# Row patches of the last quads on the GpSimd queue, and dummy matmuls in the slots of quads 13 to 15

## Chip, cores and metric

The kernel runs on one core of one Trainium2 chip. The metric is the device time of one execution in microseconds. Before the change it was 457.0 us, the median of 6 runs (455.99 to 459.12). The profiled execution took 457.49 us.

## What is computed

The input is q, k, v of shape 8 x 8 x 576 x 64, the spectral weights w_r and w_i (64 modes, 512 x 512 each) and w_ch (512 x 512), all in fp32. The first half is attention with a linear distance bias inside a window of 128 tokens. The second half mixes channels in the Fourier domain along the tokens:

```python
attn = softmax(where(0 <= rel < 128, q @ k.T / 8 - slope[h] * rel, -1e9)) @ v
x = attn.transpose(0, 2, 1, 3).reshape(8, 576, 512)
X = np.fft.rfft(x, axis=1)
Xr, Xi = X.real[:, :64], X.imag[:, :64]
Yr = einsum('bmd,mde->bme', Xr, w_r) - einsum('bmd,mde->bme', Xi, w_i)
Yi = einsum('bmd,mde->bme', Xr, w_i) + einsum('bmd,mde->bme', Xi, w_r)
Y[:, :64] = Yr + 1j * Yi          # all other modes are zero
u = x + np.fft.irfft(Y, n=576, axis=1)
out = u + maximum(u @ w_ch, 0)
```

The two spectral weights are 2 x 64 matrices of 1 MB each, so their reading takes a large part of the time.

## The kernel before

The attention stage comes first, and while it runs some spectral weights are already read. It leaves x and its spectrum XC in SBUF. The spectral stage then takes the weights in order of k = 2m + ri, where m is the mode and ri chooses w_r or w_i. A weight matrix is one load of 1 MB. Most loads go through the SyncE queue (`load_w`, L443, the issue in L456) into a ring of buffers. A weight that was just used makes room for one that comes eight later, so in the loop each slot first runs its matmuls and then issues a later load.

The loop at L791 runs over 16 quads g of four modes, and inside it over i = 0 to 7, so k = 8g + i. A slot runs four matmuls of 128x512 (L823) that add into one accumulator `acc`; each mode fills 32 of its rows (16 for the real part and 16 for the imaginary part, 8 batches each). In the last quad (g = 15, `LAST`) modes 60 and 61 go to an accumulator of their own, `half_acc`, and modes 62 and 63 are also computed transposed into `accT` by 16 small matmuls a slot (L817). After its weight, a slot has room for one more piece of work:

- `quads`: the end of an earlier quad. `quad_end` scales the accumulator (L586) and transposes it into YT. For the late quads `late_end` does it (L543 to L566): VectorE scales `acc` into a tile yq (L547), `scatter` copies its rows to the spectrum Z by DMA (L548), TensorE transposes yq (L552), and VectorE copies the transposes (L555, L560). `late_end` is called for g = 14 with four modes (56 to 59) and, after i = 3 of g = 15, for two modes (60 and 61). For g = 14 it goes on to `late_channels` (L568): four matmuls with wch, a ScalarE copy into a tile yw (L575), and `scatter` into ZW.
- `side`: from quad 8 on, 22 pieces, one on each odd slot. Four are `spectra` of the first half of the modes, 18 are `project` of one unit of tokens each (L671; its 16 matmuls are L683). The last runs on k = 107. At the end of quad 13, four more `spectra` are put in (L607, L616, copies into Z in L622); the first of them does nothing.

`scatter` (L631) issues six DMAs, one for each of batches 2 to 7. Each has 8 rows of 1 KB, or 4 rows where two modes are patched. Before the change the patches into Z go out on SyncE (L548 and L877), the patches into ZW on GpSimd (L576).

yq and yw share a tag with two buffers in the pool `fin` (bufs=2, L532). So a new one waits until one of the two last tiles is done with, its DMA reads included.

Before k = 127 the psum pool of the loop is closed, and the first matmuls of the output stage run (`begin(0)` and `add_tokens(0)`, L808 and L809). After the loop the last two modes are scaled (L872 to L876) and patched into Z (L877), then the step list of L889 forms the outputs: `activate(j)` uses ZW, `finish(j)` uses Z, and each result is written to the output by SyncE. The patch into ZW for quad 15 is issued inside `activate(0)`. The order of instructions on each engine, SyncE included, is the order of the program.

Of the kernel before, what the change touches and what calls it, by code (L numbers as in the profile page):

```python
# [10 lines left out]
FP32 = mybir.dt.float32  # L11
# [9 lines left out]
P = 128  # L21
# [379 lines left out]
def kernel(  # L401
# [10 lines left out]
    nc = tc.nc  # L412
    ctx.enter_context(tc.manual_schedule(engines=ALL | {SP}))
    B, H, S, _ = q.shape
    NM, DM, _ = moe_w_r.shape
# [8 lines left out]
    ident = const.tile([P, P], BF16, name="ident")  # L424
# [34 lines left out]
    with ExitStack() as actx:  # L459
        at = _Attention(tc, actx, q, k, v, (ident, F, FT), x, XC, raw)  # L460
        n = len(at.units)
# [11 lines left out]
        wt = at.ps.tile([P, P], FP32, tag="av", bufs=1, name="warm")  # L473
# [29 lines left out]
        for h in (0, 2):  # L503
# [4 lines left out]
        side = {0: [(at.offset, 4), (at.offset, 6), (at.decay, 5), (at.offset, 5), (at.decay, 7),  # L508
                    (at.offset, 7), (at.decay, 4), (at.decay, 6)]}
        lags = [lag for _, _, lag in STAGE]  # L510
        for stage in range(min(lags), n + max(lags)):
# [8 lines left out]
            if stage in AHEAD:  # L520
                if stage:
                    b, g = at.units[stage - 1]
# [5 lines left out]
    with ExitStack() as mctx:  # L528
# [11 lines left out]
        ps = pctx.enter_context(tc.tile_pool(name="fps", bufs=2, space=PSUM))  # L540
        heads, free = {}, []

        def late_end(acc, g, n):  # L543

            rows, m0 = slice(0, 32 * n), 4 * (g % 8)
            yq = pool.tile([P, DM], BF16, tag="yq")
            nc.vector.tensor_scalar_mul(yq[rows], acc[rows], 2.0 / S)  # L547
            scatter(nc.sync, yq, g, 0, 2 * n, lambda b: Z[:, b])  # L548
            yield
            tr = ps.tile([P, 4, P], BF16, tag="tr", bufs=1, name="tr")  # L550
            for et in range(4):
                nc.tensor.transpose(tr[:, et, rows], yq[rows, et * P : (et + 1) * P],  # L552
                                    ident[rows, rows])
            for ri in range(2):
                nc.vector.tensor_copy(  # L555
                    YT[:, 1, :, :2, m0 : m0 + n, ri],
                    tr[:, :, rows].rearrange("p e (j c) -> p e c j", c=32)[
                        :, :, 16 * ri : 16 * ri + 2])
            yT = pool.tile([P, 2, 4, P], BF16, tag="xT", name="xT")[:, 0]
            nc.vector.tensor_copy(yT[:, :, rows], tr[:, :, rows])  # L560
            heads[g] = yq, yT
            if n < 4:
                return
            yield
            zw = ps.tile([P, DM], FP32, tag="zw", bufs=1, name="zw")
            late_channels(g, zw, yT)  # L566

        def late_channels(g, zw, yT):  # L568
            for et in range(4):
                nc.tensor.matmul(zw, lhsT=yT[:, et], rhs=wch[:, et],  # L570
                                 start=(et == 0), stop=(et == 3))

            def patch():
                yw = pool.tile([P, DM], BF16, tag="yq")
                nc.scalar.copy(yw, zw)  # L575
                scatter(nc.gpsimd, yw, g, 0, 8, lambda b: ZW[:, b // 2, 1])  # L576

            if g == LAST:
                heads["patch"] = patch
            else:  # L580
                patch()
# [49 lines left out]
        def scatter(queue, rows, g, lo, hi, dst):  # L631

            for b in range(2, B):
                r = 64 * (b % 2) + 8 * (g % 8)
                queue.dma_start(out=dst(b)[r + lo : r + hi],  # L635
                                in_=rows.rearrange("(k v) e -> k v e", v=16)[lo:hi, b])
# [19 lines left out]
        def token_tiles(j):  # L656
            b, st = units[j]
            return x[:, b : b + 2, st] if st < FULL else x[:, b + 1 : b + 4 : 2, FULL]
# [3 lines left out]
        def transposed(j):  # L662
            src = token_tiles(j)
            tr = ps.tile([P, 2, 4, P], BF16, tag="tr", bufs=1, name="tr")
            for n in range(2):
                for dt in range(4):
                    nc.tensor.transpose(tr[:, n, dt], src[:, n, dt * P : (dt + 1) * P], ident)  # L667
            xTs[j] = pool.tile([P, 2, 4, P], BF16, tag="xT", name="xT")
            nc.vector.tensor_copy(xTs[j], tr)  # L669

        def project(j):  # L671

# [114 lines left out]
        quads, side, recycle = [], [], list(again)  # L787
        ZW = Z = XW = wch = w2 = None
        K1 = again[-1] + 1
        LAST = NM // 4 - 1  # L790
        for g in range(NM // 4):  # L791
            acc = (lps if g % 2 else ps).tile([P, DM], FP32, tag="acc", bufs=1, name="acc")
            if g == LAST:
                half_acc = ps.tile([P, DM], FP32, tag="z", bufs=1, name="z")
                accT = lps.tile([P, 4, 2, 32], FP32, tag="accT", name="accT")
            for i in range(8):
                m, ri = 4 * g + i // 2, i % 2
                if 2 * m + ri not in wq:
                    continue
                w = wq[2 * m + ri]  # L800
                if 2 * m + ri == 2 * NM - 1:
                    assert not side and not quads
                    pctx.close()
                    head = mctx.enter_context(
                        tc.tile_pool(name="hps", bufs=1, space=PSUM, reuse_waits="tile"))
                    heads.update(mm=[head], yy=[head])
                    free.append(0)
                    begin(0)  # L808
                    add_tokens(0)  # L809
                window = []  # L810
                for a in range(4):
                    c0 = (a // 2 * 2 * NC + 16 * (1 - ri) + a % 2 * 8) * NM + m
                    window.append(XC[:, c0 : c0 + 31 * NM + 1 : NM])
                into = half_acc if g == LAST and i < 4 else acc
                for a in range(4 if g == LAST and i >= 4 else 0):
                    for et in range(4):
                        nc.tensor.matmul(  # L817
                            accT[:, et, i // 2 - 2], lhsT=w[a][:, et * P : (et + 1) * P],
                            rhs=window[a], start=(i == 4 and a == 0 and et == 0),
                            stop=(i == 7 and a == 3 and et == 3), skip_group_check=True,  # L820
                        )
                for a in range(4):
                    nc.tensor.matmul(  # L823
                        into[32 * (i // 2) : 32 * (i // 2) + 32],
                        lhsT=window[a],
                        rhs=w[a],
                        start=(ri == 0 and a == 0), stop=(ri == (m > 0) and a == 3),
                        tile_position=(0, 32 * (i // 2)),
                    )
                k = 8 * g + i  # L830
                if recycle:
                    load_w(1, early, True, [recycle.pop(0)])
                elif homes[k] not in (early, None):
                    load_w(1, homes[k], False)
                if k == K1 - 1:
                    actx1.close()
                    w2 = mctx.enter_context(
                        tc.tile_pool(name="w2", bufs=NWB, side="right", reuse_waits="tile")
                    )
                    load_w(NWB, w2, False)  # L840
                    right = mctx.enter_context(
                        tc.tile_pool(name="late", bufs=1, side="right", reuse_waits="tile")
                    )
                    wch = right.tile([P, 4, DM], BF16, name="wch")
                    nc.gpsimd.dma_start(out=wch, in_=moe_w_ch.rearrange("(a p) e -> p a e", p=P))
                    ZW = right.tile([P, B // 2, 2, DM], BF16, name="ZW")
                    Z = right.tile([P, B, DM], BF16, name="Z")
                    XW = right.tile([P, len(units), 2, DM], BF16, name="XW")

                if quads:  # L850
                    if next(quads[0], True):
                        quads.pop(0)
                elif side and k % 2:
                    side.pop(0)()
                if g == LAST and i == 3:
                    quads.append(late_end(half_acc, g, 2))
                    next(quads[0])
            if g < LAST:
                quads.append((late_end(acc, g, 4) if g == LAST - 1 else quad_end(acc, g)))
                next(quads[0])  # L860
            if g == 7:
                side += [partial(spectra, 0, bp) for bp in range(B // 2)]
                side += [partial(project, j) for j in range(len(units))]
            elif g == LAST - 2:
                assert not side
                side += [partial(spectra, 1, bp) for bp in range(B // 2)]
# [3 lines left out]
        yq, yT = heads[LAST]  # L870
# [51 lines left out]
```

## Time and profile before

| | us |
|---|---|
| median of 6 runs | 457.0 (455.99 to 459.12) |
| profiled execution: its own time | 457.49 |
| its span, first to last instruction | 455.7 |
| PE busy in the span | 356.2 (78%) |
| DVE, ACT, POOL busy | 178.3, 151.7, 51.0 |
| DMA moved | 157.47 MB, mean 346 GB/s |

Mean granted TensorE clock: 0.873 of full speed. All times of the trace count from the start of the span. PE is TensorE, PEld its weight loads, DVE VectorE, ACT ScalarE, POOL GpSimd, SP SyncE; a q behind a name means the engine's sequencer, which waits and issues. A line such as L823 is a line of the kernel. The page cuts the span into 40 slices of 11.4 us, and a digit is a busy share in tenths. An arrow in brackets names the idle time of an engine before an instruction, and what ended it. A wait for several things is put down to the one that came last.

The weight loop is the stretch from about 151 us to 418 us; from about 422 us on the outputs are formed and written.

### The profile page before, as it was taken

The page shows a single profiled execution, that of the slowest core. Times are in us where ns is not written, and L with a number is a line of the kernel's source. Part 1 is how long each engine was busy: PE and PEld are TensorE (multiplying, and loading weights), DVE is VectorE, ACT ScalarE, POOL GpSimd, SP SyncE. Part 2 cuts the span into 40 slices and gives each one's busy share as a digit, 9 for nine tenths or more (in the row PEclk, how much of TensorE's full clock was granted, in tenths as well). Part 3 has the DMA queues.
Part 4 walks back from the last instruction along what each step waited for, and adds up shares of the span by engine and source line. Part 5 has one row for each costly group of instructions (what it writes and reads, how often), then busy time and mean ns, then how long its engine had stood idle before and what let it go on. Part 6 is the DMA issues. An engine that isn't in the chain of part 4 may idle for free.

```text
span 455.7 us, 7991 instructions
## 1 busy us (share of the span) xinstructions
PE 356.2 (78%) x3346; PEld 192.8 (42%) x3346; DVE 178.3 (39%) x325; ACT 151.7 (33%) x188; POOL 51.0 (11%) x94
## 2 busy tenths in 40 slices
PE   5797999999966534467756868999999978649993
PEld 3466776777653212112222334444444433324331
DVE  7989699998732101001010231122121211302683
ACT  6878799999800000000000110221112200100671
POOL 8610101012421100000000000000000000020610
PEclk9999899999998665556587798999999997977998
DMA  8999999999999999999999999999999999980698
GB/s 284 323 335 315 296 281 302 308 292 250 213 298 313 309 315 316 345 399 423 419 421 422 421 423 419 417 425 418 419 422 419 422 419 423 420 340 3 226 325 285
DMA packets 52307, 157.47 MB, mean 346 GB/s; under 512 B 4080, under 2 KB 23216, under 8 KB 39600
## 3 DMA queue, kind: packets, MB, share of 16 engines
q1 hardware_dynamic: 47328, 141.67, 81.0%
q0 software_dynamic: 4944, 15.31, 16.9%
q8 instruction: 26, 0.43, 0.4%
q14 instruction: 9, 0.07, 0.0%
HBM read 162.53 MB, written 9.44 MB: 377 GB/s over the span
## 4 chain that ended last, share of the span: by engine, by line
DMA 40%; PE 39%; DVE 13%; issue 3%; ACT 2%; POOL 1%; SPq 0%; DVEq 0%; ACTq 0%; POOLq 0%
DMA w<-in_moe_w_i_dram 17%; DMA w<-in_moe_w_r_dram 12%; PE acc L823 11%; PE my L683 7%; DMA vr<-in_moe_w_r_dram 7%; PE av L332 4%; PE tr L667 2%; DMA ZW<-yw 2%; PE my L645 2%; DVE x L348 2%; PE tp L251 2%; DVE vb L234 2%; DMA qr<-in_q_dram 2%; PE xt L369 2%; DVE att L306 2%
## 5 line engine op out<-in xcount | busy, mean ns | idle before, releaser
L823 PE MATMUL acc<-w,XC 128*32 128x512 bf16 x468 | 129.2, 468 | 52.1 <-DMA w<-in_moe_w_i_dram 35.2
L823 PEld LDWEIGHTS <-XC 128*32 128x32 bf16 x508 | 58.1, 141 | 122.8 <-issue 93.6
L295 ACT ACTIVATE att<-sc 128x1024 bf16<-128x1024 f32 x64 | 64.0, 1031 | 8.0 <-PE sc L285 7.9
L611 ACT CAST ZW<-zw 128x512 bf16<-128x512 f32 x7 | 4.1, 586 | 159.4 <-PE zw L607 159.4
L586 DVE TENSOR_SCALAR yq<-acc 128x512 bf16<-128x512 f32 x13 | 9.0, 689 | 104.4 <-PE acc L823 104.4
L692 ACT CAST XW<-my 128x512 bf16<-128x512 f32 x36 | 19.3, 589 | 77.9 <-PE my L645 77.9
L332 PE MATMUL av<-vb,att 128*128 128x132 bf16 (+1 forms) x576 | 38.6, 218 | 4.7 <-DVE x L348 3.0
L332 PEld LDWEIGHTS <-att 128*128 128x128 bf16 x704 | 36.8, 99 | 10.3 <-DVE x L348 7.3
L669 DVE COPY xT<-tr 128x1024 bf16<-128x1024 bf16 x18 | 12.5, 692 | 71.1 <-PE tr L667 71.1
L635 POOL DMA_DIRECT2D ZW<-yw x12 | 6.3, 533 | 261.6 <-ACT yw L575 261.6
L683 PE MATMUL my<-wch,xT 128*64 128x512 bf16 x288 | 34.5, 382 | 0.8 <-DVE xT L669 0.8
L257 ACT COPY qkT<-tp 128x1152 bf16<-128x1152 bf16 x30 | 33.5, 1117 | 3.2 <-PE tp L251 2.4
L285 PE MATMUL sc<-qkT 64*64 64x256 bf16 (+2 forms) x640 | 25.9, 271 | 2.1 <-ACT qkT L257 1.2
L348 DVE TENSOR_TENSOR x<-av,rec 128x640 bf16<-128x640 f32 x32 | 26.4, 825 | 1.1
L771 DVE TENSOR_TENSOR o<-yy,r 128x1024 f32<-128x1024 f32 (+1 forms) x20 | 22.0, 1116 | 6.4 <-ACT r L734 4.0
L285 PEld LDWEIGHTS <-qkT 64*64 64x64 bf16 x640 | 15.0, 111 | 19.7 <-issue 16.7
L683 PEld LDWEIGHTS <-xT 128*64 128x64 bf16 x288 | 14.8, 109 | 19.0 <-issue 6.9
L234 DVE CAST vb<-vr 64x1024 bf16<-64x1024 f32 x32 | 22.2, 694 | 0.2
L272 PE MATMUL sc<-bias,ident 128*128 128x512 bf16 x64 | 21.0, 412 | 1.4 <-ACT att L295 1.4
L734 ACT ACTIVATE r<-mm 128x1024 f32<-128x1024 f32 (+1 forms) x19 | 18.2, 980 | 11.4 <-PE mm L645 11.3
L306 DVE TENSOR_TENSOR att<-att,mask 128x1024 bf16<-128x1024 bf16 x32 | 20.6, 685 | 0.0
L622 DVE CAST Z<-z 64x512 bf16<-64x512 f32 x14 | 9.6, 689 | 27.5 <-PE z L616 27.4
(118 smaller groups left out, 350.1 us busy)
## 6 DMA issues: line engine op xcount, KB each, us to landing
w<-in_moe_w_r_dram SPq DMA_DIRECT2D x53, 1024.0 KB
w<-in_moe_w_i_dram SPq DMA_DIRECT2D x46, 1024.0 KB
qr<-in_q_dram SPq DMA_DIRECT2D x16, 576.0 KB
kr<-in_k_dram SPq DMA_DIRECT2D x16, 576.0 KB
vr<-in_v_dram SPq DMA_DIRECT2D x32, 256.0 KB
out_dram<-o SPq DMA_DIRECT2D x15, 512.0 KB
w<-in_moe_w_i_dram POOLq DMA_DIRECT2D x14, 512.0 KB, 23.6
w<-in_moe_w_r_dram POOLq DMA_DIRECT2D x8, 512.0 KB, 8.3
```

The lines of the kernel that those rows point to most:

```text
L234: nc.vector.tensor_copy(self.vb[u % 2][row, :, :, :, W * half : W * half + D], src[row, :2])
L257: (self.nc.vector.tensor_copy if u < 2 and w == "q" else self.nc.scalar.copy)(dst.rearrange("q h (p j) -> q h p j", j=TPP), tp.rearrange(" ...
L272: nc.tensor.matmul(sc[:, e], lhsT=self.ident, rhs=self.bias[:, hv].rearrange("p j n -> p (j n)"), start=True, stop=False, skip_group_check ...
L285: nc.tensor.matmul(sc[64 * half : 64 * half + 64, e, j * 256 + c0 : j * 256 + c0 + n], lhsT=qkT[row, 1, h, k0 + j : k0 + P : 2], rhs=qkT[r ...
L295: self.nc.scalar.activation(self.att[u % 2][:, kt * 8 * P : (kt + 1) * 8 * P], sc.rearrange("p e n -> p (e n)"), AF.Exp, scale=1.0 / math. ...
L306: nc.vector.tensor_tensor(out=rows, in0=rows, in1=self.table[:, heads], op=ALU.mult)
L332: nc.tensor.matmul(bank[:, qt * W : qt * W + rhs[j].shape[1]], lhsT=att[:, o : o + P], rhs=rhs[j], start=(n == 0 and j == 0), stop=(n == l ...
L348: nc.vector.tensor_tensor(out=self.x[:, b, :, cs].rearrange("p t (h d) -> p h t d", h=2), in0=tiles[:, :, :, :D], in1=rec.unsqueeze(-1).br ...
L683: nc.tensor.matmul(mm[ROWS[half]], lhsT=lhsT, rhs=wch[:, dt], start=(dt == 0), stop=False, skip_group_check=True,)
L692: nc.scalar.copy(XW[:, j, n], mms[n])
L771: nc.vector.tensor_tensor(out=o[:, c], in0=yy[:, c], in1=r[:, c], op=ALU.add)
L823: nc.tensor.matmul(into[32 * (i // 2) : 32 * (i // 2) + 32], lhsT=window[a], rhs=w[a], start=(ri == 0 and a == 0), stop=(ri == (m > 0) and ...
```

## The change

There are three edits. The row patches of `late_end` into Z (six DMAs for modes 56 to 59, six for modes 60 and 61) are issued by GpSimd instead of SyncE; the final patch (L877) stays on SyncE. A new function `warm` issues six matmuls of 128x512 into the two psum buffers of the tag `my`, from the identity and wch; nothing reads them. And `warm` is called in slots that have no piece of `quads` or `side`: in quad 13 once `side` is empty, and in quads 14 and 15, except for k = 127.

```diff
@@ late_end
             nc.vector.tensor_scalar_mul(yq[rows], acc[rows], 2.0 / S)
-            scatter(nc.sync, yq, g, 0, 2 * n, lambda b: Z[:, b])
+            scatter(nc.gpsimd, yq, g, 0, 2 * n, lambda b: Z[:, b])
             yield
@@ before project
+        def warm():
+            for _ in range(6):
+                wt = ps.tile([P, DM], FP32, tag="my", bufs=2, name="my")
+                nc.tensor.matmul(wt, lhsT=ident, rhs=wch[:, 0], start=True, stop=True)
@@ the loop over i
                 elif side and k % 2:
                     side.pop(0)()
+                elif g > LAST - 2 and k < 2 * NM - 1 or g == LAST - 2 and not side:
+                    warm()
                 if g == LAST and i == 3:
```

## Prediction

> **What bounds the kernel now.** I read the page's slices first. DMA is at its ceiling until slice 35 and PE is nearly full. Then comes a hole: slice 36 has no DMA, and PEclk has fallen to half there.
>
> ```profile
> PE   5797999999966534467756868999999978649993
> PEclk9999899999998665556587798999999997977998
> DMA  8999999999999999999999999999999999980698
> ```
>
> So between the weight stream and the output stream (about 404 to 422 us) neither stream sets the time. The chain of waits says what does. Columns: start, duration, step.
>
> ```profile
> 398.26 2.20 POOL ZW L635 x5
> 400.46 0.46 issue
> 400.92 6.37 DMA ZW<-yw
> ...
> 407.67 0.69 DVE yq L547
> 408.37 0.05 issue
> 408.41 0.39 PE tr L552 x4
> 408.80 1.03 PE accT L817 x16
> 409.83 1.85 PE acc L823 x4
> ...
> 419.99 1.54 DMA Z<-yq
> 421.53 0.58 ACT yw L575
> ```
>
> The scaling of modes 60 and 61 (yq, L547) has its sums by 401.1 and starts at 407.67: its buffer is one of two (tag yq), held by a tile that a patch transfer still reads. Which one? The wait names ZW<-yw, the patch of the tile after the last yq, not the last yq itself. And the second yw (421.53) follows a wait for Z<-yq. So the two tiles swapped buffers. The only order that gives this is that a buffer goes to whoever comes when it is free, first freed first: the older yq was still held by its row patches on SP. The SP timeline shows those going out singly between weight landings, at 394.53, 395.3, 397.53, 400.02, 402.50, and
>
> ```profile
> 405.49 0.56 SPq L635 DMA_DIRECT2D Z<-yq  x1
> ```
>
> whereas the six of yw on POOL take 3.19 us from 398.26. SP's own waits book these pauses to DMA w: a patch waits until an earlier weight has landed.
>
> PE's timeline gives the prices. [...]
>
> ```profile
> 368.08 3.18 PE L823 MATMUL acc<-w,XC 128*32 128x512 bf16 x16
> 372.69 1.07 PE L823 MATMUL acc<-w,XC 128*32 128x512 bf16 x4 [1.42 <-DMA w<-in_moe_w_r_dram]
> ...
> 390.10 1.07 PE L823 MATMUL acc<-w,XC 128*32 128x512 bf16 x4 [1.42 <-DMA w<-in_moe_w_i_dram]
> 391.09 1.04 PE L607 MATMUL zw<-wch,YT 128*128 128x512 bf16 x4
> 391.97 0.39 PE L616 MATMUL z<-ident,YT 128*128 128x128 bf16 x4
> ...
> 408.41 0.39 PE L552 MATMUL tr<-ident,yq 64*128 64x64 bf16 x4 [3.73 <-DVE yq L547]
> ```
>
> Four weight matmuls take 0.99 (390.10 to 391.09), four 128x512 matmuls with wch take 0.88, so 0.22 each. Weights land every 2.49 us. Last, the granted clock by stretch:
>
> ```profile
> 368.00:377.00 9.00, 5.70 (x30) 2.89 (x29) 1.19 (x3) 1.05 (x2) 0.00 (x0) 1.00 1.01 422
> 377.00:384.00 7.00, 5.72 (x16) 2.00 (x15) 0.00 (x0) 0.13 (x1) 0.00 (x0) 0.53 1.02 424
> 385.00:404.00 19.00, 12.81 (x72) 6.52 (x71) 4.75 (x9) 1.76 (x3) 3.19 (x6) 1.00 1.02 418
> 405.00:415.00 10.00, 6.59 (x48) 3.24 (x48) 1.14 (x4) 0.00 (x0) 0.00 (x0) 0.50 0.37 138
> ```
>
> (After the span and five busy times come granted clock, DMA share, GB/s.)
>
> **Part 1: row patches to POOL.** Removed from SP: 12 issues (six for modes 56 to 59, six for 60 and 61). No later SP work gains: its last weight issue is at 391.19, its next work, the final patch, at 418.35. Added to POOL: 12 x 0.53 = 6.4 us, where it is otherwise idle from 401.45 to 422.40. The first six go out within 3.2 us of the scaling. Their landing has no row; the nearest are yw's six beside the same weights: 5.8, 6.1, 6.4 us from issue (least, median, most). The DMA side could be nothing different (bytes and engines are the same) or up to a few tenths lost by the weights: k = 125 landed 2.99 us after 124 (405.49 against 402.50) while both patches ran, 0.5 over the pitch. That loss exists now; I take no change.
>
> If the scaling of modes 56 to 59 ends near 395.3 (worked out below), the last of six is issued at 397.9 and lands at 404.3. The older yq buffer is then freed before yw's, so the next yq takes it and can start at about 404.3. PE reaches its transposes only at 405.0. The wait of 3.73 is gone. Next late is the weight itself: k = 125 is there at 405.49.
>
> The skill speaks against this part ("DMA: Bandwidth & Descriptors", Issuing engines are not separate DMA queues): issuing from more engines saves only the issuing sequencer's time, usually small. By it the move is worth nothing. By the row, SP's issuing takes 11.5 us (394.53 to 406.05) because each patch waits for a weight, against 3.2 on POOL. I follow the row.
>
> **Part 2: dummies.** The branch is reached in 11 slots: k = 108 to 111 (side work ended at 107), 114, 116, 118, 122, 123, 125, 126. Six 128x512 matmuls each: 66 in all. One slot costs 6 x 0.22 = 1.32 us at full clock, 1.35 with the change of weights; a half clock would double it. The first takes the psum of the last projections, whose copies end at 369.05, before PE gets there: no stall. Nothing reads the result. [...]no row shows a cost; I take none.
>
> Are they in idle slots? Only partly. At 368.08 PE is behind: 16 matmuls run through, for weights that had landed from 362.7 on (372.69 less 4 x 2.49); the lag shrinks to zero just at k = 111. With dummies it does not. The walk at full clock, each step from the rows above:
> - k = 108 to 111: 4 x (0.99 + 1.35) = 9.4, to 377.5. Four weights now go one by one; today two of them overlap.
> - 112 with its transposes 1.4, to 378.9. 113 and 114 (other array columns, may overlap: 1.0 to 2.0, I take 1.5) and 1.35, to 381.7.
> - 115 and 117, weight and spectrum (0.99 + 0.88 + 0.40) 2.27 each; 116 and 118, 2.35 each: to 391.0, 0.9 behind the 390.10 of now.
> - From 119 to 120 3.74 as now (VectorE's Z copies), from 120 to 122 3.5 as now: 398.2. DVE ends the mode 56 to 59 scaling at about 395.3.
> - 122 and 123, 2.35 each: 402.9. 124 takes 2.1 (402.53 to 404.61 now), 405.0; transposes 0.4, 405.4. Each weight has landed by then.
> - 125: lands 405.5; 2.1 + 1.35, to 408.95. 126 the same, to 412.4.
> - Begin and token matmuls before k = 127: 1.0 now (414.49 to 415.50): 413.4.
>
> Today k = 127 starts at 415.50, so it comes 2.1 us earlier. Of the two terms: the vanished wait gives 408.73 - 405.5 = 3.2; the slots of 125 and 126 cost 3.45 instead of 2.88 at half clock, together -1.1. The dummies cost more there than the clock gives. What follows (scaling, final patch, yw, outputs) hangs on k = 127 in the same order at clock 1.0, and shifts whole. The lag costs no bandwidth: SP issues a weight up to 19.7 us before it is there (k = 127: 391.19 to 410.85), and a lag of 5 us leaves most of that.
>
> Here the skill has a rule too ("TensorE: Matmul & The Clock Gate", Why this matters for your kernels): no idle gaps over about 3 us, and the clock holds. By it, with the 3.73 wait gone, full clock comes free and the dummies of 125 and 126 are a loss of 2.7. The row disagrees: before the fall at 377 no gap exceeds 1.42, PE was merely 63% busy. Yet at 67% (385 to 404) it held. Without dummies the last slots would cost 2.1 to 2.9, with them 3.45, by either reading.
>
> **The sum.** The profiled execution took 457.49 (span 455.7, 1.8 around it). Less 2.1, rounded to 2.0 for small waits: 455.5. The median of the runs, 457.0, is 0.5 lower, so 455.0.
>
> **Rivals.**
> 1. *Main case, 0.60*: gain 1 to 3, 454.0 to 456.0; the spread is the slot (1.30 to 1.40 eleven times), the overlap of 113 and 114, and k = 125's landing.
> 2. *The dummies hide, 0.08*: if k = 127 waited only for its weight (SP's patch queue shows that landing at 410.85), 4.6 less: near 452.5. Against it: 125 and 126 are 6.9 us of PE work after 405.5.
> 3. *A wash, 0.15*: patches of POOL land 2 us later than yw's, because 12 follow each other and DVE copies beside them; yq starts at 406.5, gain gone: 457.0.
> 4. *Slower, 0.17*: the yq of modes 60 and 61 still gets yw's buffer. yw's patches now queue on POOL behind six others, and if POOL too holds only eight in flight (SP's pauses fit eight: seven weights and one patch), the third waits for the first patch to land, about 401.1. The last goes out at 402.9, lands at 409.3; yq 409.7 to 410.4, transposes to 410.8, then 6.9 + 1.0: k = 127 at 418.7, +3.2, 460.2. Without that limit +2.1. For it: today's wait names yw. Against it: the swap shown above. It costs from a yq start of 406.5 on, and over 0.5% from 408.8.
>
> **How the numbers follow.** About 0.5% (2.3 us) is what a measurement here can tell from no change. Faster by more: case 2 and nearly half of case 1, 0.35. Slower by more: case 4, with a tail of 3, 0.19. The rest 0.46. Range 453.0 to 459.2: it reaches into case 4 and leaves out its far end and most of case 2. The main case alone is 454.0 to 456.0.
>
> **What would show it.** Right: yq L547 starts near 404.5; six Z<-yq on POOL near 395; granted clock 1.0 from 368 to 425; k = 120 near 394.7; k = 127 at 413.4; 66 more matmuls of 0.22 spacing. Wrong: yq after 406.5 (case 3 or 4); clock 0.5 anywhere after 404, which would make each last slot about 5.5 us; k = 122 much later than 398.2, which would mean that the lag of the dummies is larger than walked.

## Result and the profile after

The changed kernel takes 454.96 us (median of 16 runs, 452.37 to 456.35); beside it the kernel before takes 457.59 (35 runs). The ratio is 0.9938, 95% interval 0.992 to 0.9956: faster by 0.44 to 0.8%. The forecast was 455.0 from 457.0, a ratio of 0.9956. The profiled execution took 454.02 (span 452.2), 3.5 less than the one of before, where the medians differ by 2.6: single executions scatter. In the traces of the 12 kernels of this document k = 122 starts anywhere from 396.4 to 398.3. So the span is split below at the starts of k = 122, 124 and 127. One run of all those below, of the kernel with five slots, fell in a slower state (457.69 us, the other five 450.60 to 452.92), and the median given for that kernel leaves it out.

The page's slices of the changed kernel:

```profile
PE   5797999999966624457566678999999999889993
PEclk9999899999999665565766899999999999999998
```

From slice 23 on the clock is whole until the outputs are nearly done, and PE has no hole in slice 35. The windows say the same (columns as before the change: span, five busy times, granted clock, DMA share, GB/s):

```profile
368.00:377.00 9.00, 9.00 (x38) 3.45 (x36) 0.69 (x1) 0.00 (x0) 0.00 (x0) 1.00 1.01 421
377.00:384.00 7.00, 6.76 (x36) 3.31 (x36) 1.88 (x4) 0.58 (x1) 0.00 (x0) 1.00 1.02 426
385.00:404.00 19.00, 16.30 (x84) 7.38 (x83) 4.07 (x8) 1.75 (x3) 6.32 (x12) 1.00 1.02 408
405.00:415.00 10.00, 9.77 (x83) 5.57 (x82) 0.94 (x7) 0.00 (x0) 3.29 (x6) 1.00 0.41 148
```

VectorE's timeline gives the scaling of modes 60 and 61. It comes 3.1 us earlier (407.67 before), and it now waits for the older yq's patches:

```profile
404.53 0.68 DVE L547 TENSOR_SCALAR yq<-z 64x512 bf16<-64x512 f32 x1 [8.33 <-DMA Z<-yq]
```

GpSimd's timeline shows the twelve patches (Z<-yq) and the six of yw among them:

```profile
395.37 3.17 POOL L635 DMA_DIRECT2D Z<-yq  x6 [237.80 <-DVE yq L547]
398.54 1.04 POOL L635 DMA_DIRECT2D ZW<-yw  x2
400.94 1.66 POOL L635 DMA_DIRECT2D ZW<-yw  x3 [1.36 <-DMA Z<-yq]
402.88 0.53 POOL L635 DMA_DIRECT2D ZW<-yw  x1 [0.27 <-DMA Z<-yq]
405.50 3.29 POOL L635 DMA_DIRECT2D Z<-yq  x6 [2.10 <-DVE yq L547]
```

Eight issues, then a pause until the first patch has landed (400.66): this queue too holds eight. Rival 4 was right on that. It was wrong on the buffer: yq no longer waits for yw. PE's timeline has the start of k = 122 and the slots of the last quad. Before:

```profile
397.55 1.07 PE L823 MATMUL z<-w,XC 128*32 128x512 bf16 x4 [0.25 <-DMA w<-in_moe_w_r_dram]
...
402.53 1.10 PE L817 MATMUL accT<-XC,w 128*128 128x32 bf16 x16 [1.42 <-DMA w<-in_moe_w_r_dram]
...
415.50 1.09 PE L817 MATMUL accT<-XC,w 128*128 128x32 bf16 x16
```

After:

```profile
397.72 1.07 PE L828 MATMUL z<-w,XC 128*32 128x512 bf16 x4 [0.23 <-DMA w<-in_moe_w_r_dram]
...
403.36 1.09 PE L822 MATMUL accT<-XC,w 128*128 128x32 bf16 x16 [0.49 <-DMA w<-in_moe_w_r_dram]
...
405.95 1.09 PE L822 MATMUL accT<-XC,w 128*128 128x32 bf16 x16 [0.23 <-DMA w<-in_moe_w_i_dram]
...
408.03 1.47 PE L674 MATMUL my<-wch,ident 128*128 128x512 bf16 x6
409.34 1.09 PE L822 MATMUL accT<-XC,w 128*128 128x32 bf16 x16
...
413.59 1.09 PE L822 MATMUL accT<-XC,w 128*128 128x32 bf16 x16
```

k = 127 starts at 413.59 (walked: 413.4). The split:

| us | before | after | difference |
|---|---|---|---|
| start of k = 122 | 397.55 | 397.72 | +0.17 |
| k = 122 to k = 124 | 4.98 | 5.64 | +0.66 |
| k = 124 to k = 127 | 12.97 | 10.23 | -2.74 |
| k = 127 to the end of the span | 40.2 | 38.6 | -1.6 |

The first row is the scatter of the stages ahead. The second is the change's doing: it is 4.97 to 4.99 in all six kernels here that issue the row patches on SP, and 5.43 to 5.72 in all six that issue them on POOL, so the weights come later beside the patches. The second and third together are -2.1, which is what was walked.

The last row was not in the forecast: I had the rest "shift whole". It does so up to the patch of quad 15 into ZW (called the final patch below), which goes out 6.90 after the start of k = 127 in both. Then unit 5, the first that reads it, starts 11.00 after k = 127 before the change, after a wait, and 9.85 after it with the change. That is 1.15 of the 1.6. PE's timeline of before, and of after:

```profile
426.50 0.57 PE L645 MATMUL mm<-ZW,FT 64*64 64x512 bf16 x4 [0.99 <-DMA ZW<-yw]
```

```profile
423.44 0.39 PE L645 MATMUL mm<-ZW,FT 64*64 64x512 bf16 x4
```

The bytes of this patch and its queue are the same in both kernels. Of the DMA answers for the 4.1 us from its first issue, only the one of before has a row for instructions. (A row for issues gives KB each and the median us to landing; q8 carries instructions: packets, MB, share.) Before, then after:

```profile
q8 instruction: 1, 0.02, 1.5%
...
ZW<-yw POOLq DMA_DIRECT2D x6, 8.0 KB, 3.6
```

```profile
ZW<-yw POOLq DMA_DIRECT2D x6, 8.0 KB, 2.1
```

In the trace of before one packet of 16384 bytes of instructions (a fetch) starts at 424.46 and takes 0.96 us. A DMA reports its end by 16 completion marks. Of those of the patch's first DMA, fifteen come between 424.54 and 424.74, the sixteenth at 426.46, and PE goes on at 426.50. After the change the fetches start at 410.16 and 428.34, and no mark is late (422.60 to 422.79). The dummies had put 132 instructions (66 matmuls with their weight loads) into PE's stream.

### The profile page after: what moved, and what is told of

It reads as the page before. It is cut to its first block, busy times and chain, and to the rows that moved or that the text cites. A ratio compares the mean times of both kernels' runs of the same rounds, so it can differ in the third digit from the quotient of the medians.

```text
span 452.2 us, 8128 instructions
## 1 busy us (share of the span) xinstructions
PE 363.0 (80%) x3412; PEld 196.7 (44%) x3412; DVE 178.2 (39%) x325; ACT 151.6 (34%) x188; POOL 57.3 (13%) x106
## 4 chain that ended last, share of the span: by engine, by line
DMA 41%; PE 40%; DVE 13%; issue 2%; ACT 2%; POOL 0%; DVEq 0%; SPq 0%; POOLq 0%; ACTq 0%
DMA w<-in_moe_w_i_dram 30%; PE acc L828 10%; PE my L688 7%; DMA vr<-in_moe_w_r_dram 7%; PE av L332 4%; DMA w<-in_moe_w_r_dram 3%; PE tr L667 2%; PE my L645 2%; DVE vb L234 2%; DVE x L348 2%; PE tp L251 2%; PE yy L749 2%; DMA qr<-in_q_dram 2%; PE yy L762 2%; DVE q L239 2%
## 5 line engine op out<-in xcount | busy, mean ns | idle before, releaser
L828 PE MATMUL acc<-w,XC 128*32 128x512 bf16 x468 | 124.2, 454 | 48.6 <-DMA w<-in_moe_w_i_dram 34.8
L332 PE MATMUL av<-vb,att 128*128 128x132 bf16 (+1 forms) x576 | 38.8, 219 | 4.8 <-DVE x L348 3.1
L635 POOL DMA_DIRECT2D Z<-yq x12 | 6.5, 544 | 239.9 <-DVE yq L547 239.9
L688 PEld LDWEIGHTS <-xT 128*64 128x64 bf16 x288 | 14.8, 109 | 18.9 <-issue 6.9
```

The source lines that it names most:

```text
L332: nc.tensor.matmul(bank[:, qt * W : qt * W + rhs[j].shape[1]], lhsT=att[:, o : o + P], rhs=rhs[j], start=(n == 0 and j == 0), stop=(n == l ...
L688: nc.tensor.matmul(mm[ROWS[half]], lhsT=lhsT, rhs=wch[:, dt], start=(dt == 0), stop=False, skip_group_check=True,)
L828: nc.tensor.matmul(into[32 * (i // 2) : 32 * (i // 2) + 32], lhsT=window[a], rhs=w[a], start=(ri == 0 and a == 0), stop=(ri == (m > 0) and ...
```

## Experiments

Three theories stood after this. Theory 1, mine: the vanished wait gives the gain up to k = 127, the dummies of the last slots cost more than their clock gives, and the last 1.3 us come from where an instruction fetch falls. Theory 2: the clock that the dummies hold makes the gain. Theory 3: the final patch lands sooner because patches left SP for POOL. Every run has five rounds against the kernel before. "To k = 127" is from the start of k = 124; "tail" is from the start of k = 127 to the end of the span. These columns and the landing are of one profiled execution each.

| kernel | ratio, 95% interval | median us | to k = 127 | fetch during the final patch; its median landing | tail |
|---|---|---|---|---|---|
| before | 1 | 457.59 | 12.97 | yes; 3.6 | 40.2 |
| changed | 0.9938 (0.992 to 0.9956) | 454.96 | 10.23 | no; 2.1 | 38.6 |
| patches alone | 0.9963 (0.994 to 0.9986) | 455.75 | 10.34 | yes; 4.4 | 40.7 |
| dummies alone | 1.0008 (0.9985 to 1.0031) | 457.5 | 14.18 | no; 2.1 | 38.8 |
| before, stream shifted by 132 | 0.9975 (0.9952 to 0.9999) | 456.07 | 12.00 | no; 2.1 | 38.8 |
| before, stream shifted by 256 | 0.9997 (0.997 to 1.0024) | 458.13 | 13.58 | yes; 3.1 | 40.0 |
| three buffers | 0.9948 (0.9922 to 0.9975) | 454.47 | 10.00 | yes; 3.7 | 41.4 |
| three buffers, shifted by 132 | 0.9867 (0.9839 to 0.9894) | 452.84 | 9.25 | no; 2.2 | 38.9 |
| patches, shifted by 132 | 0.9894 (0.987 to 0.9918) | 453.92 | 9.29 | no; 2.2 | 38.7 |
| changed, none in 125 and 126 | 0.9872 (0.9837 to 0.9908) | 452.48 | 8.40 | no; 2.2 | 38.6 |
| changed, five slots | 0.9888 (0.9845 to 0.9931) | 452.04 | 8.53 | no; 2.2 | 38.1 |
| nine slots, three buffers | 0.9876 (0.9848 to 0.9904) | 452.28 | 8.52 | no; 2.2 | 38.6 |

The runs were made in three sets, beside which the kernel before had medians of 457.26 (patches alone, dummies alone, 132, three buffers), 458.17 (256, the two combinations, none in 125 and 126) and 458.81 (the last two rows). So the ratios compare better than the medians.

**Patches alone.** The changed kernel without its call of `warm`:

```diff
-                elif g > LAST - 2 and k < 2 * NM - 1 or g == LAST - 2 and not side:
-                    warm()
```

> The move of the row patches alone, no dummy matmuls. Theory 1 (the gain is the vanished wait of yq L547, the dummies only cost, and the last 1.3 us of the changed kernel's gain come from where PE's instruction fetch falls): yq starts near 404.5, k = 125 near 405.9, k = 127 near 412.0 (clock held) to 412.7 (half clock), against 415.50; the instruction fetch stays at the same place of the program, so the final patch ZW<-yw takes its 4 us; about 454.1 to 454.8. Theory 2 (the clock held by the dummies makes the gain): about 457.6, clock 0.5 from 405 to 415. Theory 3 (the final patch lands sooner because the earlier patches left SP or used POOL's queue): as theory 1, but the final patch takes 2.3 us, and 452.8 to 453.5.

yq started 2.1 after k = 124 (405.59), against 1.2 in the changed kernel, and k = 125 3.20 after k = 124. The clock fell, at 404.0, and k = 127 came 10.34 after k = 124, as in the changed kernel. So up to k = 127 the move gives the whole gain (from k = 122 it is 2.2, and 2.1 in the changed kernel), and all 66 dummies together give nothing that shows. One execution of each cannot tell more: kernels with the same code at the end differ by about 1 us in this column (patches alone and with the shift 10.34 and 9.29, before and its two shifts 12.00 to 13.58). The final patch took 4.4 us although the other patches were on POOL: Theory 3 falls.

```profile
q8 instruction: 1, 0.02, 1.5%
...
ZW<-yw POOLq DMA_DIRECT2D x6, 8.0 KB, 4.4
```

**Dummies alone.** The changed kernel with `scatter(nc.sync, ...)` in `late_end`:

```diff
-            scatter(nc.gpsimd, yq, g, 0, 2 * n, lambda b: Z[:, b])
+            scatter(nc.sync, yq, g, 0, 2 * n, lambda b: Z[:, b])
```

> The dummies alone, row patches stay on SP. Theory 1: yq waits for yw's patch again and starts near 407.7, k = 127 near 416.5 where the clock holds, near 420 where it falls; the fetch is shifted as in the changed kernel, so the final patch takes 2.3 us: 457 to 461. Theory 2: k = 127 earlier than 415.50, about 455. Theory 3: the final patch takes 4 us: 458.5 to 462.

VectorE's waits name yw's patch again, and PE pays for it, then for dummies of which the first set runs partly at half clock:

```profile
DVE yq L547 <- DMA ZW<-yw: 10.8, 1, 10.8
```

```profile
408.34 0.29 PE L552 MATMUL tr<-ident,yq 64*128 64x64 bf16 x4 [2.89 <-DVE yq L547]
408.56 1.09 PE L822 MATMUL accT<-XC,w 128*128 128x32 bf16 x16
...
411.43 1.96 PE L674 MATMUL my<-wch,ident 128*128 128x512 bf16 x6
413.23 1.08 PE L822 MATMUL accT<-XC,w 128*128 128x32 bf16 x16
```

k = 127 comes 1.2 later than before, the tail is 1.4 shorter, and the time is that of before. Theory 2 falls: the dummies without the move gain nothing.

**The stream shifted by 132 and by 256 instructions.** Nothing at the end is changed; short matmuls that nothing reads are put in slots where PE waits for weights (k = 33 to 44; for 256, eight in each of 16 slots of k = 33 to 50):

```diff
+        def shift():
+            for _ in range(6):
+                wt = ps.tile([P, DM], FP32, tag="my", bufs=2, name="my")
+                nc.tensor.matmul(wt[:, :P], lhsT=ident, rhs=ident, start=True, stop=True)
...
+                elif 33 <= k < 45 and k != 40:
+                    shift()
```

> The kernel before, with 66 short matmuls (128x128, not read) in slots k = 33 to 44, where PE waits for weights: nothing but PE's place in its instruction stream is changed for the end. Theory 1: the 16 KB instruction fetch no longer falls at 424.5; the final patch takes about 2.3 instead of 4.1 us; k = 127 as before; about 1.3 us less, 456.3. Theory 3: no change, 457.6, final patch 4 us.

> The kernel before, with 128 short matmuls (256 PE instructions, 16 KB) in 16 slots of k = 33 to 50: a whole fetch of 16 KB more. If the place of the fetch is what moved the final patch (Theory 1), it is back at about 424.5 and the patch takes 3.6 to 4.1 as before: 457.3, no gain, though there are more dummies than in the run with 66. Rival (early matmuls help by themselves, by the clock or by filling PE): at least the gain of 66, 456.0 or less, and a patch of about 2.1.

With 132 the fetch that fell at 424.46 starts at 409.4, the patch takes 2.1, and the tail is 38.8. With 256 it is back at 424.3, the patch takes 3.1, the tail 40.0 and the time is that of before. The DMA answer with 256:

```profile
q8 instruction: 1, 0.02, 1.3%
...
ZW<-yw POOLq DMA_DIRECT2D x6, 8.0 KB, 3.1
```

More instructions do not help; their place does. A period of 256 instructions fits packets of 16384 bytes: from 155 us on, PE in the trace of before starts 243 to 277 instructions, weight loads included, between two of them, 256 on average. The ratio of this shift alone and that of the patches alone multiply to 0.9938, that of the changed kernel, though each has an interval about as wide as its gain.

The fetch ahead of this one matters too. In before it starts at 401.32 and takes 1.10 us, while the six row patches of yw, on which yq waits, are in flight. Their sixteenth marks come 0.7 to 0.9 after the fifteenth; with the shift by 132 no fetch lies there, and it is 0.0 to 0.1. The DMA answers for the 9.2 us from the first issue, before and then shifted by 132:

```profile
q8 instruction: 1, 0.02, 0.7%
...
ZW<-yw POOLq DMA_DIRECT2D x6, 8.0 KB, 6.1
```

```profile
ZW<-yw POOLq DMA_DIRECT2D x6, 8.0 KB, 5.4
```

The first six patches on POOL land after a median of 6.1 to 6.4 us in the five kernels with a fetch among them (before, shifted by 256, patches alone, three buffers, five slots), and of 5.3 to 5.6 in the seven others. yq starts 5.1 after k = 124 in before and 5.4 with 256, but 4.4 with 132 and 4.3 with the dummies alone. So about 0.7 to 0.9 of yq's wait before the change was the fetch's, not the buffer's. The dummies of the changed kernel moved this fetch too (to 389.0): the later yq of the patches alone, whose fetch starts at 401.71, fits that.

**Three buffers.** The kernel before with bufs=3 at all three places of the tag (the yq of `quad_end` and yw as well); patches on SP:

```diff
-            yq = pool.tile([P, DM], BF16, tag="yq")
+            yq = pool.tile([P, DM], BF16, tag="yq", bufs=3)
```

> The kernel before with three buffers instead of two for the tag of yq and yw; patches stay on SP, no dummies. Theory 1: yq of modes 60 and 61 needs no wait for a patch, it starts near 401.3; k = 127 near 412 to 412.7; final patch 4 us; about 454.1 to 454.8, as with the patches moved. Theory 2: about 457.6. If the place of the row patches itself (behind the weights) were what costs, no gain either.

VectorE now waits for the sums alone:

```profile
DVE yq L547 <- PE z L823: 5.1, 1, 5.1
```

yq starts 1.4 ahead of k = 124, and k = 127 comes 10.00 after it, with the patches still behind the weights. So it was the held buffer that cost, not where the row patches stand. From k = 122, which counts the weights' delay, k = 127 comes after 14.98, against 15.77 for the patches alone and 15.87 in the changed kernel. Of the tail of 41.4, 0.6 is not the final patch's: the clock was still half when k = 127 began, and the patch goes out 7.53 after it, not 6.90.

**Patches or three buffers, with the shift.** Two kernels that add the 132 shifted instructions to the ones above.

> Patches on POOL, no dummies at the end, but 66 short matmuls in slots k = 33 to 44 that only shift PE's instruction stream. Theory 1: k = 127 about 10.3 after k = 124 at half clock, as with the patches alone; the final patch takes about 2.1 instead of 4.4; so as fast as the changed kernel, about 454.5, which would mean that the dummies' clock is worth nothing and their number is. Rival (the dummies gain by the clock at the end): stays at the 455.8 of the patches alone.

> Three buffers for yq and yw, patches on SP, no dummies at the end, 66 short matmuls in slots k = 33 to 44. Theory 1: the two gains add: k = 127 about 10.0 after k = 124, final patch 2.1 instead of 3.7: about 453.2, faster than the changed kernel. If they do not add: 454.5, as with three buffers alone.

Both gain at the tail, 2.0 and 2.5 us (0.6 of the latter is the clock), more than the 1.3 expected; by medians of different sets of runs 1.8 and 1.6. Patches with a shift are at least as fast as the changed kernel, without a dummy in the last quads. They gain 1.05 and 0.75 ahead of k = 127 as well. That is the clock: it came back at 410.6 and 409.2 here, at 414.2 and 413.9 in the kernels without the shift. In both pairs the time from k = 126 to k = 127 alone shrank by 1.05 or more. Whether the shift has a part in that is open.

**Fewer dummies.** `k < 2 * NM - 4` in place of `k < 2 * NM - 1` leaves out those of 125 and 126; without the second half of the condition those of quad 13 go too; the last kernel has nine slots and three buffers.

> The changed kernel without the dummies of k = 125 and 126 (54 instead of 66). Theory 1 (dummies on the path cost what they last): with the clock held by the nine earlier slots, k = 126 starts when its weight has landed, about 5.4 after k = 124, and k = 127 about 8.7 after k = 124 instead of 10.2: 1.5 us less than the changed kernel, about 453.3. If the clock falls all the same at 404 as it did with the patches alone: k = 127 about 10.3 after k = 124, equal to the changed kernel. Instruction fetch falls 24 instructions later than in the changed kernel, outside the final patch, which takes about 2.1.

> The changed kernel with dummies in k = 114, 116, 118, 122, 123 alone (30 of 66). Theory 1: those of quad 13 only delay PE there and add nothing later, so k = 127 again about 8.4 after k = 124 with the clock held at the end; the stream is shifted by 60 PE instructions, the fetch that fell at 423 with the patches alone comes about 4 us earlier, ahead of the final patch: 0.988 of before. If the dummies of quad 13 are needed for the clock of the last quad: 0.5 from about 404, k = 127 about 10.3 after k = 124.

> Patches on POOL, three buffers for yq and yw, dummies in nine slots (not in 125 and 126). Theory 1: yq starts as soon as k = 123 is summed, about 1.4 before k = 124; the weight's landing then ends the wait for k = 125 as it does with two buffers on POOL, so k = 127 stays about 8.2 to 8.4 after k = 124 and the time is that of the run without the last two dummies (about 0.988 of before). If the buffer still cost something there: up to 1 us less.

The clock held in all three up to k = 127 and beyond. The windows from 395 to 403 and from 404 to 414, of the patches alone, and then without the dummies of 125 and 126:

```profile
395.00:403.00 8.00, 4.89 (x22) 2.06 (x20) 0.64 (x4) 0.58 (x1) 5.66 (x11) 1.00 1.02 401
404.00:414.00 10.00, 9.67 (x66) 4.60 (x65) 1.13 (x4) 0.00 (x0) 3.82 (x7) 0.50 0.48 179
```

```profile
395.00:403.00 8.00, 6.99 (x41) 3.19 (x40) 0.00 (x0) 0.59 (x1) 5.45 (x11) 1.00 1.02 391
404.00:414.00 10.00, 8.65 (x76) 5.02 (x75) 1.29 (x7) 0.59 (x1) 3.30 (x6) 1.00 0.41 149
```

k = 127 came 8.40 after k = 124, 1.83 less than in the changed kernel; by medians of different sets of runs the time is 2.5 less. Dummies in five slots and the third buffer change nothing more: 8.5 in both, and k = 126 now waits for its weight in all three. All three beat the kernel before. Two also lie clear of the changed kernel; the interval of the five slots (up to 0.9931, and widest of all) reaches into its own. The two combinations above, which have no dummy at the end, stand level with these three: all five have ratios of 0.987 to 0.989, the intervals overlap, and from k = 122 to k = 127 they take 14.1 to 14.2 with the held clock on POOL, 14.2 with three buffers on SP and a half clock, 14.8 with the patches on POOL and a half clock. So in these traces the held clock is worth 0.6 to 0.8 beside patches on POOL, and the runs cannot rank the five.

## Why the prediction was right, point by point

- *The buffers.* The swap read from the two waits was right: yq took the older yq's buffer and started at 404.53 (forecast about 404.3). The third buffer shows that this wait was the cost. The first patch went out at 395.37 (forecast 395.3).
- *The issuing rule* (the Trainium skill, "DMA: Bandwidth & Descriptors", Issuing engines are not separate DMA queues) against the row: the row was right on the gain. Patches alone are faster by 0.14 to 0.6%, since what SP's waits held was a buffer, not time of the issuing engine.
- *The dummies' walk.* The six dummies of a slot take 1.31 to 1.40 in the trace (408.03 to 409.34, 411.41 to 412.81) against 1.35. k = 120 at 394.02 (394.7), k = 122 at 397.72 (398.2), k = 126 at 409.34 (408.95), k = 127 at 413.59 (413.4). PE was ahead of the walk up to 122, in part by chance: k = 108 began at 366.23, not at 368.08. Then it waited for weights, which I had as landed.
- *The price of the last dummies.* Without those of 125 and 126, the two slots take 2.7 (0.6 of it a wait for a weight) and 2.1 (forecast 2.1 to 2.9) instead of 3.4 and 3.5.
- *The clock rule* (the Trainium skill, "TensorE: Matmul & The Clock Gate", Why this matters for your kernels): patches alone have no PE gap over 1.8 us from 385 to 404, less than the 3 us that the rule allows, and the clock fell all the same. The trace of before was the better guide. PE had been busy 61% from 395 to 403 (4.89 of 8.00), and 87% in the kernel where it held.
- *A term put at zero:* the patches on POOL beside the weights, and the fetch inside yw's row patches, whose landing I took as the price of a patch. The weights went at 408 GB/s from 385 to 404 instead of 418. Weights k = 123, 124 and 125 came 2.68, 2.96 and 2.59 apart where the pitch is 2.49, together 0.3 more than the landings of before (8.23 against 7.94).
- *The step that failed:* "What follows hangs on k = 127 in the same order at clock 1.0, and shifts whole." It was 1.6 us shorter. I had costed each dummy's time on PE, and not that 132 more instructions move the fetches, one of which lay on this path. The walk to k = 127 was right (2.1); the error behind it is three quarters as large and helped. That 455.0 was met to 0.04 is luck: the tail was shorter, the base of the runs was 0.6 higher than I knew, and the medians differ by 2.6 where the two profiled executions differ by 3.5.

## What to carry to other kernels

When a wait names a DMA, ask first which tile's buffer the waiting instruction takes over, and when the other buffers come free; one more buffer is the cheaper cure where it fits. Fillers for the clock, if they pay at all, belong in slots that wait for data, none on the stretch that nothing else hides. Before a change of a few tenths of a per cent is explained by what it does, look where instruction fetches fall: a shift of the stream alone, by unused instructions far ahead, tells the two apart.

## What the hardware showed unexpectedly

One 16 KB packet of instructions, 0.96 us on the DMA engines, delayed a patch of 48 KB by 1.0 to 2.3 us (median landing 3.1 to 4.4 with it, 2.1 to 2.2 without, in 12 kernels without exception, one trace of each), and lengthened the tail by 1.1 us and more (40.0 to 41.4 against 38.1 to 38.9). Among the weights such a packet cost row patches 0.5 to 1.1 us. Of a DMA's sixteen completion marks only the last was late in the trace of before, which fits one engine of the sixteen being held up; that it is that engine was inferred from the times. Why the mark is 1.7 us late, more than the packet takes, is open. With the patches alone, the clock fell to half at 404.0, after 8 us (395 to 403) in which PE was busy 61% with no gap over 1.8 us.
